# A gated long-convolution and MLP stack: an on-chip re/im swap issued by one engine's DMA queue instead of two, with a new instruction plan

## The chip, the cores and the metric

The kernel runs on one core of one Trainium2 chip. A core has five engines with an in-order instruction stream each: TensorE (PE in the profile, with its weight loads as PEld), VectorE (DVE), ScalarE (ACT), GpSimd (POOL) and SyncE (SP). They share one on-chip memory of 128 partitions (SBUF, here one array called `ar` and a small one called `sm`), and the matmul accumulators (PSUM, `ps`, used as eight banks of 512 f32 per partition). Engines wait for each other through semaphores. Copies between memories, and copies within the on-chip memory, are DMAs: an instruction in an engine's stream issues them, and they then run beside the engines. The metric is the device time of one execution in microseconds.

## The reference

The sequence has 2048 tokens of 512 channels, in bf16; the MLP's hidden size is 1376. Cut to what matters:

```python
def A(q, k, v, shift_k, ssm_k, ssm_D):      # gated long convolution
    k_shift = sum(k_pad[:, t:t+S] * shift_k[:, 3-t] for t in range(4))   # causal, 4 taps
    kv = k_shift * v
    y = irfft(rfft(pad(kv, 2*S)) * rfft(pad(ssm_k, 2*S)))[:S]            # causal, 2048 taps
    return q * (y + kv * ssm_D)
def B(x):                                   # MLP
    return gelu(layernorm(x) @ w1 + b1) @ w2 + b2

x = q
x = x + A(layernorm(x), k, v, shift_k, ssm_k, ssm_D)
x = x + B(layernorm(x))
x = x + A(layernorm(x), k, v, shift_k, ssm_k, ssm_D)
x = x + B(layernorm(x))
```

Only the gate `q` differs between the two uses of A, so the convolution's result is computed once and used in both layers.

## The kernel before, in words

**The planner.** The program is written as a list of operations. `P.op` records each with the engine or engines that may run it, an assumed duration, what it reads and writes, and its PSUM tiles. `schedule` (L188) then places them one after another on the five engines in a modelled time: by a priority, which is the length of the work that follows, plus a stage's boost, plus a table of per-operation corrections ("nudges", at the end of the kernel function). Where an operation allows ACT or DVE, as PSUM evacuations and layer norms do, this choice is made there too, and so is the PSUM bank. The result is a fixed order for each engine. `sync` adds the semaphore waits that this order needs, and `emit` writes the streams. So an assumed duration or a nudge is no instruction, but it can change where any instruction stands. For DMAs the planner keeps one time, `dma_free`, at which the shared DMA engines are done with what was issued, at an assumed 400 bytes per ns (L289, L290).

**The convolution.** The sequence is cut into two halves of 1024 tokens. Each half and each half of the convolution kernel is transformed by a two-stage Fourier transform done as matmuls against tables: `stage1` (L627) and `stage2` (L641), each group of matmuls followed by an evacuation from PSUM (L541 on ACT, L542 on DVE). In a spectrum, 64 partitions hold real parts and 64 hold imaginary parts. A complex product needs each spectrum also with the two exchanged. For the convolution kernel's spectra this exchange is done by DVE copies, `swap_v` (L666). For the spectrum of the second half's `kv` it is done by DMAs, `swap` (L646 to L651): C5 is copied to C1 with partitions 0 to 63 and 64 to 127 exchanged, in two pieces of the channel axis, and in two directions for each piece, thus four DMAs of 0.5 MB, all issued through `dma` (L522). The direction `h` picks the issuing engine: SP for `h` = 0, ACT for `h` = 1. The spectral products follow on DVE (`tt`, L531): for the second half a loop over four groups, in which C5 and then C1 is multiplied by C3 and added to C6 and C4. `inverse1` (L679) and `inverse2` (L694) transform back. The short convolution is done on PE for the first half (`taps`) and on DVE for the second (`shift`).

**The MLP blocks.** The two layers run in eight blocks of 512 tokens, k = 0 to 7. In (layer, token group) they are (0,0), (0,1), (1,0), (1,1), (0,2), (0,3), (1,2), (1,3): the first half of the sequence goes through both layers before the second half, so blocks 0 to 3 run while the second half's convolution is still being computed between them. A block has four tiles of 128 tokens. For each tile there are statistics on DVE (L884, L886) with a small power on POOL (L892), a norm on ACT (L931) or DVE (L932), the product with y and the addition to x (L974, L975, shown under the line of `tt`), the statistics and a norm again, and a transpose that brings channels onto partitions. Block 0 transposes on PE. Blocks 1 to 7 use one transposing DMA for each tile, issued by SP (L986), 28 in all. Then come the first matmuls (L1009) in eleven slices of the hidden size, with a gelu on ACT for each slice (L1014), the second matmuls (L1029) for each tile, and the addition to x on DVE (L1033). The outputs leave by DMAs on SP.

So SP's stream holds the loads, then the transposes of each block, with two of the four swap DMAs among them, and then the outputs. ACT's stream holds evacuations, norms and gelus, with the other two swap DMAs among them.

Of the kernel before, what the change touches and what calls it, by code (L numbers as in the profile page):

```python
# [7 lines left out]
ALU = mybir.AluOpType  # L8
# [37 lines left out]
class Prog:  # L46
# [141 lines left out]
    def schedule(self, nudge={}):  # L188
# [32 lines left out]
        while done < n:  # L221
# [64 lines left out]
                left -= k  # L286
            free[e] = s + d
            if o.dma:
                dma_free = max(dma_free, s + d) + o.bytes / 400.0  # L289
                o.end = dma_free + (1900.0 if o.dma is True else o.dma)  # L290
            else:
                o.end = s + d
            for tl in o.tile:
# [122 lines left out]
                getattr(block, e)(body)  # L416


WF, SPL, NA1, NDX, KP, KM, SG, PG, PSW, PLN, END = 8, 1, 0, 64, 2, 0, 1, 1, 0, 0, 1
S, D, FF = 2048, 512, 1376  # L420
B = 1024
EPS = 1e-5
# [39 lines left out]
def bass_interleave_layers__ssm_conv_h3__mixer_channel_mlp__prompt_kernel(  # L462
        nc, A_q, A_k, A_v, A_shift_k, A_ssm_k, A_ssm_D, B_x, B_w1, B_b1, B_w2, B_b2, out):
    P = Prog(nc)
# [5 lines left out]
    def A(p0, n, off, *dims):  # L470
        return bass.AP(ar, p0 * AR + off, [[AR, n]] + [list(d) for d in dims])
# [4 lines left out]
    def Q(tile, p0, n, off, *dims):  # L476
        return bass.AP(ps, p0 * 4096 + tile.base * 512 + off, [[4096, n]] + [list(d) for d in dims])
# [43 lines left out]
    def dma(dst, src, nbytes, reads=(), prio=0.0, writes=None, eng=SP):  # L521
        return P.op(eng, lambda e: e.dma_start(dst, src, allow_slow_non_contiguous=True), 550.0, reads=reads,  # L522
                    writes=[dst] if writes is None else writes, dma=True, nbytes=nbytes, prio=prio, order=HOLD[0])
# [6 lines left out]
    def tt(o, a, b, op, dur, eng=DVE):  # L530
        return P.op(eng, lambda e: e.tensor_tensor(o, a, b, op), dur, reads=[a, b], writes=[o])  # L531
# [114 lines left out]
    def swap(dst0, src0, dg0=0, nd=64):  # L646
        out = []
        for h in range(2):
            s = A(64 * h, 64, src0 + dg0 * 128, [1, nd * 128])
            out.append(dma(A(64 - 64 * h, 64, dst0 + dg0 * 128, [1, nd * 128]), s, nd * 37500, reads=[s], eng=(SP, ACT)[h]))  # L650
        return out  # L651

    def W32(p0, n, off, nd, nk):
# [14 lines left out]
    def DG(r, g):  # L668
        return A(0, 128, r + 2048 * g, [1, 2048])

    def inverse1(p1, p2, z, hf, d8s):
        for d8 in d8s:
            tl = Tile(cv[hf], 0, hi[hf])
            ins = [(i, j, A(0, 128, p + (8 * d8 + i) * 128, [1, 128]), A(0, 128, R_U + 128 * j, [1, 128]))
                   for i in range(8) for j, p in enumerate((p1, p2))]

            def f(e, ins=ins, tl=tl):
                for i, j, w, m in ins:
                    r = e.matmul(Q(tl, 0, 128, i * 128, [1, 128]), w, m, start=j == 0, stop=j == 1)  # L679
                return r  # L680
            P.op(PE, f, 16 * 57.0, reads=[x for y_ in ins for x in y_[2:]], tile=tl, ni=32)
            evac(A(0, 128, z + 1024 * d8, [8, 8], [64, 16], [1, 8]),
                 lambda tl=tl: Q(tl, 0, 128, 0, [128, 8], [8, 16], [1, 8]), tl)

    def inverse2(z, y, hf):
        nd = 512
        for a2, na in [(0, 1), (1, 1)] * (NA1 > hf) + [(i, 2) for i in range(NA1 > hf, 4)]:
            tl = Tile(one if na == 1 else cv[hf], 0, hi[hf])
            ins = [(i, ri, A(0, 128, R_T2 + ((na * a2 + i) * 2 + ri) * 128, [1, 128]),
                    A(0, 128, z + ((na * a2 + i) * 2 + ri) * 64, [1024, 8], [1, 64])) for i in range(na) for ri in range(2)]  # L690

            def f(e, ins=ins, tl=tl):
                for i, ri, w, m in ins:
                    r = e.matmul(Q(tl, 0, 128, i * nd, [1, nd]), w, m, start=ri == 0, stop=ri == 1)  # L694
                return r
            P.op(PE, f, 2 * na * nd * 0.422, reads=[x for y_ in ins for x in y_[2:]], tile=tl, ni=4 * na)
            evac(A(0, 128, y + a2 * na * 512, [512, na], [1, nd]), lambda tl=tl, na=na: Q(tl, 0, 128, 0, [nd, na], [1, nd]), tl,
                 dur={ACT: 475.0, DVE: 630.0} if na == 1 else EVD)
# [130 lines left out]
    stage1([(R_H0, 0), (HT1, 256)], R_SH, 1, range(8))  # L829

    P.boost, EV[0] = FIRST, (ACT, DVE)
    inverse1(C1, C4, C6, 0, range(8))
    inverse2(C6, YS[0], 0)


# [18 lines left out]
        stage2(C1, C5, 1, g)  # L854
    for i in range(2):
        swap(C1, C5, 32 * i, 32)
    for g in range(4):
        for i, (p, x) in enumerate(((C6, C5), (C4, C1))):
            m = A(0, 128, R_H0 + 2048 * i, [1, 2048])
            tt(m, DG(x, g), DG(C3, g), ALU.mult, 1133.0)  # L860
            tt(DG(p, g), DG(p, g), m, ALU.add, 1133.0)
    inverse1(C6, C4, C1, 1, range(8))
    inverse2(C1, YS[8], 1)


    EV[0] = (ACT, DVE)
# [86 lines left out]
    for L, b in [(0, 0), (0, 1), (1, 0), (1, 1), (0, 2), (0, 3), (1, 2), (1, 3)]:  # L953
# [8 lines left out]
        bo = dict(P.boost)  # L962

        def lean(i):
            P.boost = {e: bo[e] + (3e5 if k < SPL and i < 2 else 0.0) for e in bo}
        for i, s in enumerate(sl):
            lean(i)
            zt = zts[i]
# [2 lines left out]
            if i % 2:  # L971
# [1 line left out]
                x2 = A(0, 128, XS[s - 1], [1, 1024])  # L973
                tt(z2, z2, A(0, 128, YS[s - 1], [1, 1024]), ALU.mult, 610.0)  # L974
                tt(x2, x2, z2, ALU.add, 610.0)  # L975
        lean(0)
        mr = stats(sl[:2], True, k > 0)
        lean(2)
        mr = mr + stats(sl[2:], True, k > 0)
        for i, s in enumerate(sl):  # L980
            lean(i)
            z = ntmp()
            norm(s, mr[i], A(0, 128, z, [1, 512]))
            if k not in BYPE:
                zs, xt = A(0, 128, z, [1, 512]), A(0, 128, R_XT + (k % 2) * 2048 + i * 128, [512, 4], [1, 128])
                P.op(SP, lambda e, zs=zs, xt=xt: e.dma_start(xt, zs, transpose=True), 1200.0, reads=[zs], writes=[xt],  # L986
                     dma=1250.0, nbytes=1000)
                continue
            tl = Tile(ptr, lo)
            src = [A(0, 128, z + 128 * j, [1, 128]) for j in range(4)]  # L990

            def f(e, src=src, tl=tl):
                for j in range(4):
                    r = e.transpose(QB(tl, 0, 128, 128 * j, [1, 128]), src[j], IDN)
                return r
            P.op(PE, f, 4 * 60.0, reads=src + [IDN], tile=tl, prio=2e5, ni=8)
            evac(A(0, 128, R_XT + (k % 2) * 2048 + i * 128, [512, 4], [1, 128]),
                 lambda tl=tl: QB(tl, 0, 128, 0, [128, 4], [1, 128]), tl, dur={ACT: 510.0, DVE: 360.0})
        P.boost = bo
        nt = 256 if k < SPL else 512  # L1000
        for t0, fc in [(t0, fc) for t0 in range(0, 512, nt) for fc in range(11)]:
            rows = 128 if fc < 10 else 96
            tl = Tile(pm1, lo)
# [36 lines left out]
                o = (b // 2) * B * 512 + (s % 8 - 1) * 512  # L1040
                outs.append(dma(dr(out, o, [8 * 512, 128], [1, 1024]), src, 1 << 18, reads=[src], writes=[]))
    P.schedule({
        4: -2722000, 5: -2787700, 6: -1724800, 7: -1209900, 9: -3195100, 10: -2512200, 11: -3537200, 12: -9892100,
        13: -3275900, 14: -2545200, 15: -1219700, 17: -1775500, 18: -4912800, 50: 1831800, 51: 669200, 53: 971300,
        59: 177000, 60: -127200, 63: 78900, 64: -2944000, 69: 1351300, 71: 2209900, 72: 1484900, 73: 364500,
        75: 4879100, 83: -6452800, 87: -79900, 89: -6939400, 100: -473600, 109: 505300, 112: -1220500, 130: -292500,
        139: 2217400, 144: 726100, 146: 725300, 148: 104200, 150: 46100, 152: 701300, 156: 809900, 157: 79000,
        159: 809400, 160: 1509400, 161: 1511900, 181: 2148200, 182: -4908700, 208: -675200, 216: -541300,
        217: -635900, 218: -377200, 219: -300000, 231: -2087100, 232: -1420500, 236: -1145000, 238: -1105300,
        239: -323000, 263: 1329100, 286: -314700, 323: -3260500, 325: -4484200, 333: -695800, 337: -731700,  # L1050
        358: -186700, 364: 881800, 371: 845700, 374: 5603900, 376: 7181700, 378: 5920300, 380: 8518000,
        383: -2852800, 388: 4950600, 390: 9651700, 392: 6143000, 394: 5859400, 400: -256900, 402: -359100,
        404: 4316100, 406: 4317000, 408: -231500, 410: 4127200, 412: 4968900, 416: 2718700, 420: -567700,
        423: -882600, 428: 1119900, 430: -113000, 432: -196900, 434: -57500, 445: -1125900, 449: -3768000,
        450: -1182200, 459: -2467500, 469: -1401400, 485: 614700, 487: 240000, 489: 615700, 491: 251700,
        500: -685500, 501: -2286200, 505: 413200, 508: -715300, 524: -461900, 525: -358200, 559: -2269500,
        560: -2008000, 562: -2155300, 564: -2546100, 576: 2300300, 577: 3514400, 578: 3193800, 580: 4805700,
        585: 2437100, 586: 4776600, 587: 5927400, 589: 4099400, 641: -1729200, 645: -2893000, 649: 1567700,
        675: -1125900, 750: -4094700, 758: -8732500, 795: -16699900, 797: -15253500, 799: -7825800, 801: -4476400,
        803: -19174100, 805: -16887100, 807: -13420200, 809: -14748800, 811: -13422400, 813: -13127700,  # L1060
        815: -11697300, 821: -6064400, 909: 673900, 991: -10275500})
    P.sync()
    P.emit(outs)

# [27 lines left out]
```

## Time and profile before

| | us |
|---|---|
| device time, four runs | 249.57, 251.95, 251.08, 252.67 |
| median | 251.52 |
| the profiled execution, device time | 249.57 |
| its span in the profile | 247.5 |
| evacuations on ACT (L541), 91 | 87.9 |
| gelus on ACT (L1014), 99 | 61.1 |
| norms on ACT (L931), 28, and on DVE (L932), 36 | 21.8 and 13.9 |
| elementwise products on DVE (L531), 76 | 77.0 |
| first and second MLP matmuls on PE (L1009, L1029) | 78.8 and 78.1 |
| swap DMA, issue to landing, median, from SP and from ACT | 7.4 and 9.1 |
| transposing DMA (28), issue to landing, median | 2.5 |

The profile is of one execution. Its granted clock is 1.0 throughout. Times inside it are microseconds from the span's start. Letters stand for engines as above; SPq and ACTq are the streams of SP and ACT with the DMAs that they issue; `ar<-ar` is a DMA or an operation within the on-chip memory, `ps` is PSUM. A group line gives the operation, its count, busy time and the mean of one in ns, and then the engine's idle time just before the group's instructions with what ended most of it.

### The profile page before, as it was taken

The numbers are of one execution on the slowest core, as the hardware profiler recorded it, in microseconds if no ns is written. First come the engines' busy times: TensorE is split into PE (matmuls) and PEld (weight loads), VectorE is DVE, ScalarE is ACT, GpSimd is POOL, SyncE is SP. The second block draws the span as 40 slices with busy tenths as digits, with TensorE's granted clock in tenths as the row PEclk, the third lists the DMA queues.
The fourth block names the chain that finished last, engine by engine and source line by source line (L and its number), as shares of the span: only waits on it lengthen the run. The fifth ranks groups of instructions, "written<-read, shape, count | busy, mean of one in ns | idle before, by whom it ended". The sixth has DMA issues, their size and how long they took to land.

```text
span 247.5 us, 5560 instructions
## 1 busy us (share of the span) xinstructions
PE 234.4 (95%) x2380; PEld 141.6 (57%) x2404; DVE 193.3 (78%) x362; ACT 167.9 (68%) x219; POOL 26.9 (11%) x32
## 2 busy tenths in 40 slices
PE   7999987999799999999699999999999999999995
PEld 4777776896587654456344576444444444444443
DVE  3698999999999999899999998889146966942022
ACT  3497789999999887867685399836804823743810
POOL 0001100000412010402113003111101011020000
PEclk9999999999999999999999999999999999999999
DMA  6999990604001430002692400052400030033002
GB/s 187 375 422 415 402 302 15 236 15 162 3 3 21 171 64 3 0 3 48 151 226 45 119 11 0 3 109 62 85 3 0 1 73 12 3 64 106 0 3 85
DMA packets 22097, 24.78 MB, mean 100 GB/s; under 512 B 15956, under 2 KB 17849, under 8 KB 20665
## 3 DMA queue, kind: packets, MB, share of 16 engines
q1 hardware_dynamic: 21752, 23.34, 29.8%
q10 hardware_dynamic: 320, 1.09, 1.9%
q8 instruction: 19, 0.31, 0.5%
q14 instruction: 6, 0.04, 0.0%
HBM read 16.56 MB, written 2.10 MB: 75 GB/s over the span
## 4 chain that ended last, share of the span: by engine, by line
PE 81%; ACT 11%; DVE 4%; issue 1%; DMA 1%
PE ps L1009 31%; PE ps L1029 30%; ACT ar L541 11%; PE ps L641 4%; PE ps L627 4%; PE ps L679 3%; PE ps L606 2%; PE ps L568 2%; PE ps L694 1%; DVE ar L542 1%; PE ps L759 1%; PE ps L765 1%; DMA ar<-ar 1%; DVE ar L611 1%; PE ps L586 1%
## 5 line engine op out<-in xcount | busy, mean ns | idle before, releaser
L541 ACT ACTIVATE ar<-ps 128x1024 bf16<-128x1024 f32 (+2 forms) x91 | 87.9, 1028 | 20.5 <-PE ps L641 5.6
L1014 ACT ACTIVATE ar<-ps,sm 128x512 bf16<-128x512 f32 (+2 forms) x99 | 61.1, 640 | 40.8 <-PE ps L1009 40.2
L1009 PE MATMUL ps<-ar 128*128 128x512 bf16 (+3 forms) x387 | 78.8, 355 | 2.5 <-DMA ar<-ar 2.0
L531 DVE TENSOR_TENSOR ar<-ar 128x2048 bf16<-128x2048 bf16 (+2 forms) x76 | 77.0, 1049 | 2.7 <-ACT ar L541 1.9
L1029 PE MATMUL ps<-ar 128*128 128x512 bf16 (+2 forms) x351 | 78.1, 372 | 0.7 <-issue 0.2
L1009 PEld LDWEIGHTS ps<-ar 128*128 128x128 bf16 (+1 forms) x396 | 38.8, 100 | 37.7 <-DMA ar<-ar 1.9
L1029 PEld LDWEIGHTS ps<-ar 128*128 128x128 bf16 (+1 forms) x363 | 34.8, 98 | 38.1
L1033 DVE TENSOR_TENSOR ar<-ar,ps 128x512 bf16<-128x512 bf16 (+1 forms) x33 | 21.7, 668 | 33.6 <-PE ps L1029 33.5
L892 POOL TENSOR_TENSOR sm<-sm 128x2 f32<-128x2 f32 (+1 forms) x24 | 25.4, 1060 | 178.3 <-DVE sm L891 177.8
L884 DVE BATCH_NORM_STATS2 sm<-ar 128x6 f32<-128x512 bf16 x64 | 42.3, 682 | 0.3
L931 ACT ACTIVATE ar<-ar,sm 128x512 bf16<-128x512 bf16 x28 | 21.8, 808 | 4.8 <-DMA ar<-ar 2.0
L627 PE MATMUL ps<-ar 128*64 128x128 bf16 x640 | 22.4, 221 | 1.5 <-ACT ar L541 1.0
L627 PEld LDWEIGHTS ps<-ar 128*64 128x64 bf16 x640 | 18.6, 110 | 6.7 <-issue 2.6
L641 PE MATMUL ps<-ar 128*128 128x64 bf16 x512 | 18.6, 193 | 3.6 <-ACT ar L541 1.9
L641 PEld LDWEIGHTS ps<-ar 128*128 128x128 bf16 x512 | 16.8, 98 | 7.4 <-ACT ar L541 3.7
L679 PE MATMUL ps<-ar 128*128 128x128 bf16 x256 | 15.6, 219 | 0.2 <-DVE ar L531 0.2
L679 PEld LDWEIGHTS ps<-ar 128*128 128x128 bf16 x256 | 14.7, 98 | 1.8 <-DVE ar L531 0.4
L932 DVE TENSOR_SCALAR ar<-ar,sm 128x512 bf16<-128x512 bf16 x36 | 13.9, 414 | 1.0 <-DMA ar<-ar 0.5
L666 DVE COPY ar<-ar 64x2048 bf16<-64x2048 bf16 x16 | 10.9, 688 | 0.4
L886 DVE BATCH_NORM_AGGREGATE sm<-sm 128x2 f32<-128x6 f32 x64 | 10.2, 174 | 0.4
L542 DVE CAST ar<-ps 128x1024 bf16<-128x1024 f32 x8 | 9.7, 1217 | 0.1
L694 PE MATMUL ps<-ar 128*128 128x512 bf16 x32 | 7.9, 380 | 0.0
(33 smaller groups left out, 64.9 us busy)
## 6 DMA issues: line engine op xcount, KB each, us to landing
ar<-tab_s SPq DMA_DIRECT2D x4, 1024.0 KB, 18.1
ar<-in_A_ssm_k_dram SPq DMA_DIRECT2D x4, 512.0 KB, 6.7
ar<-in_A_q_dram SPq DMA_DIRECT2D x2, 1024.0 KB, 6.0
ar<-in_A_v_dram SPq DMA_DIRECT2D x2, 1024.0 KB, 10.0
out_dram<-ar SPq DMA_DIRECT2D x7, 256.0 KB, 2.2
ar<-in_A_k_dram SPq DMA_DIRECT2D x1, 1408.0 KB, 7.6
ar<-in_B_w_dram SPq DMA_DIRECT2D x1, 1376.0 KB, 22.1
ar<-in_B_w_dram SPq DMA_DIRECT2D x1, 1280.0 KB, 23.0
```

The source lines that it names most:

```text
L531: return P.op(eng, lambda e: e.tensor_tensor(o, a, b, op), dur, reads=[a, b], writes=[o])
L541: return e.activation(dst, src(), AF.Copy)
L627: r = e.matmul(Q(tl, 64 * ri, 64, i * 128, [1, 128]), w, m, start=j == 0, stop=j == len(terms) - 1)
L641: r = e.matmul(Q(tl, 0, 128, i * nd, [1, nd]), w, m, start=True, stop=True)
L679: r = e.matmul(Q(tl, 0, 128, i * 128, [1, 128]), w, m, start=j == 0, stop=j == 1)
L884: P.op(DVE, lambda e, st=st, x=x: e.bn_stats(st, x), 630.0, reads=[x], writes=[st])
L892: P.op(POOL, lambda e: e.tensor_tensor(r, v, h, ALU.pow), 1200.0, reads=[v, h], writes=[r])
L931: return e.activation(o, x, AF.Identity, bias=mr[2], scale=mr[1])
L1009: r = e.matmul(Q(tl, 0, rows, 0, [1, nt]), w, m, start=dk == 0, stop=dk == 3)
L1014: P.op(ACT, lambda e, dst=dst, tl=tl, rows=rows, bias=bias, nt=nt: e.activation(dst, Q(tl, 0, rows, 0, [1, nt]), AF.Gelu_apprx_tanh, bias= ...
L1029: r = e.matmul(Q(tl, 0, 128, 0, [1, n]), ins[fc][0], ins[fc][1], start=fc == 0, stop=fc == 10)
L1033: P.op(DVE, lambda e, x=x, tl=tl, n=nc2: e.tensor_tensor(x, x, Q(tl, 0, 128, 0, [1, n]), ALU.add), 85.0 + nc2 * 1.055, reads=[x], writes=[ ...
```

## The change

The swap's `h` = 0 direction goes to ACT too, so that all four swap DMAs are issued by ACT, and SP issues only the transposes, besides loads and outputs. In the planner's model, a DMA marked 1251.0 instead of 1250.0 neither waits for nor adds to `dma_free`; the transposes are so marked. The table of nudges is a new one throughout, so the plan is made anew: the order on each engine, and for some operations the choice between ACT and DVE. `inverse1` takes its spectra as a tuple; called with two, it issues what it issued before. The switches `IA` and `ST4` are 0 and `SPS` is (0,), with which the added branches issue what the code before issued.

```diff
@@ schedule
             if o.dma:
-                dma_free = max(dma_free, s + d) + o.bytes / 400.0
-                o.end = dma_free + (1900.0 if o.dma is True else o.dma)
+                if o.dma == 1251.0:
+                    o.end = s + d + o.dma
+                else:
+                    dma_free = max(dma_free, s + d) + o.bytes / 400.0
+                    o.end = dma_free + (1900.0 if o.dma is True else o.dma)
...
-WF, SPL, NA1, NDX, KP, KM, SG, PG, PSW, PLN, END = 8, 1, 0, 64, 2, 0, 1, 1, 0, 0, 1
+WF, SPL, NA1, NDX, KP, KM, SG, PG, PSW, PLN, END, SPS, ST4, IA, SWA = 8, 1, 0, 64, 2, 0, 1, 1, 0, 0, 1, (0,), 0, 0, 1
...
@@ swap
-            out.append(dma(A(64 - 64 * h, 64, dst0 + dg0 * 128, [1, nd * 128]), s, nd * 37500, reads=[s], eng=(SP, ACT)[h]))
+            out.append(dma(A(64 - 64 * h, 64, dst0 + dg0 * 128, [1, nd * 128]), s, nd * 37500, reads=[s], eng=(ACT if SWA else SP, ACT)[h]))
...
@@ transposes of the MLP input
                 P.op(SP, lambda e, zs=zs, xt=xt: e.dma_start(xt, zs, transpose=True), 1200.0, reads=[zs], writes=[xt],
-                     dma=1250.0, nbytes=1000)
+                     dma=1251.0 if SWA else 1250.0, nbytes=1000)
...
@@ P.schedule({ ... }), first lines of the table
-        4: -2722000, 5: -2787700, 6: -1724800, 7: -1209900, 9: -3195100, 10: -2512200, 11: -3537200, 12: -9892100,
+        4: -2868200, 5: -1791300, 8: 340900, 9: -3663100, 10: -643600, 11: -4939200, 12: -9800600, 13: -5002900,
...
```

## The prediction

> **What bounds the kernel now.** I read the page's busy times, then a table of windows, then the chain of work, then each queue's own timeline where the chain leaves the matmuls.
>
> ```profile
> PE 234.4 (95%) x2380; PEld 141.6 (57%) x2404; DVE 193.3 (78%) x362; ACT 167.9 (68%) x219; POOL 26.9 (11%) x32
> ...
> 10.00:42.00 32.00, 29.53 (x641) 24.49 (x643) 29.93 (x52) 26.86 (x29) 2.18 (x3) 1.00 0.85 328
> 42.00:69.00 27.00, 24.24 (x525) 20.02 (x523) 26.63 (x37) 27.00 (x29) 3.57 (x4) 1.00 0.28 95
> 69.00:118.00 49.00, 48.01 (x503) 29.87 (x507) 46.91 (x82) 40.89 (x63) 6.89 (x6) 1.00 0.16 41
> 118.00:154.00 36.00, 33.75 (x255) 19.41 (x257) 35.11 (x66) 25.77 (x36) 5.97 (x5) 1.00 0.39 92
> 154.00:247.00 93.00, 90.45 (x424) 42.47 (x430) 51.03 (x121) 44.13 (x64) 8.02 (x10) 1.00 0.17 40
> ```
>
> The windows give length, then busy us of PE, PEld, DVE, ACT and POOL, the clock, and DMA. PE looks busy everywhere, but from 42 to 69 us ACT is busy for 27.00 of 27.00 and DVE for 26.63: those two set the pace there. DVE stays above 95% until 154. From 154 to the end it has slack, and PE alone decides. So a delay in what DVE or ACT must finish before an MLP block moves the end; after that only PE's own gaps count. The chain shows one gap, just where block 2 (the first after both halves of token group 0 are done) begins:
>
> ```profile
> 117.12 0.36 DVE ar L1033
> 117.47 2.48 DMA ar<-ar
> 119.95 0.27 issue
> 120.23 9.45 PE ps L1009 x43
> ```
>
> The change speaks of the DMA queues, so I read SP and ACT around it:
>
> ```profile
> 113.61 5.12 SPq L986 DMA_TRANSPOSE ar<-ar  x4
> 119.55 1.17 SPq L522 DMA_DIRECT2D ar<-ar  x2
> 132.38 5.12 SPq L986 DMA_TRANSPOSE ar<-ar  x4
> ...
> SPq L986 <- ACT ar L931: 13.3, 2, 12.3
> ...
> 119.56 1.83 ACTq L522 DMA_DIRECT2D ar<-ar  x2
> 121.44 0.69 ACT L1014 ACTIVATE ar<-ps,sm 128x512 bf16<-128x512 f32 x1 [1.91 <-PE ps L1009]
> 122.02 0.80 ACT L931 ACTIVATE ar<-ar,sm 128x512 bf16<-128x512 bf16 x1
> ...
> L522 SPq DMA_DIRECT2D ar<-ar x2: 543/565/587, 119.5 to 120.1; - x2
> L522 ACTq DMA_DIRECT2D ar<-ar x2: 535/898/1260, 119.6 to 120.1; - x2
> ```
>
> Block 2's four transposes stand before the swap on SP. They are 1.28 us apart because SP issues them one after another (5.12 us for four), and the last lands 2.5 us after its issue: 117.45 + 2.5 = 119.95, which is the gap. The next four, block 3's, stand behind the swap, but SP waited 12.3 us for ACT's norm (L931), long after its two swap issues were over at 120.7. **The swap delays no transpose here.** ACT is the opposite: its first gelu of block 2 starts at 121.44, right behind its two swap issues, though its matmuls were done before.
>
> [...] four 0.5 MB pieces from two queues took up to 11.1 us to land, with the DMA engines 94% busy from 120 to 130. So I give the queue itself no bandwidth. [...]
>
> **The change, part by part.** I take the instruction order of both programs. The new switches (SPS, ST4, IA) stand at values that issue what was issued before, and the planner's case 1251 acts only through the order it gives. Operations and their number are the same, except that three norms (L931/L932) move from DVE to ACT, one stage-1 evacuation from ACT to DVE, and one small K evacuation back.
>
> 1. *Two swap issues leave SP* (0.57 us each). SP then waited 12.3 us anyway: gain 0. If that cover went, 1.2 us.
>
> 2. *Two more swap issues go on ACT*, four in a row, behind block 2's first gelu. Two took 1.83 us. Four cost between 4 x 0.57 = 2.3 us (SP's pace) and 4 x 1.31 = 5.2 us (ACT's slower one, with the gap to the next instruction). I take S = 3.0: the slow one came while SP was issuing too, which it no longer does. Queued behind them on ACT are the other ten gelus of block 2 and block 3's first norm. The matmul group of each hidden slice takes 0.86 us. The waits of the new program let six groups run before the seventh needs the second gelu. The last swap source evacuation ends, by step 4, some 1.3 us after block 2's first matmul; then gelu 0.6, the issues S, gelu 0.67 and about 0.15 of signalling: the second gelu is seen at 1.3 + 0.6 + 3.0 + 0.8 = 5.7 us, against six groups, 5.2. PE waits 0.5 to 0.6 us (0 for S = 2.3; 2.8 for 5.2). Before, it waited 0.2 here. Net **+0.4**.
>
> 3. *A new order up to 69 us.* Nothing is added but 0.7 us more on DVE (evacuation 1.12 to 1.2 in, norms 0.33 each and small evacuations about the same out). K arrives one 1 MB table later, about 2.5 us at 410 GB/s, and PE has 48 more stage-1 matmuls ahead of it. Charging each DVE instruction what it took before, DVE starts the spectral products at about 42.0 against 41.89. ACT then has 26.7 us to the first MLP evacuation, as before. **0**, within 1.5 either way.
>
> 4. *When block 2 can start.* Three things must be there. (a) DVE's last addition of block 1 (L1033), which frees a PSUM bank: 106.25 us of DVE work lie ahead of it before, and it started at 117.12, so DVE had paused 10.9 us in all; 108.37 us lie ahead in the new order, as bn_stats of blocks 4 and 5 (0.60 each) are pulled forward. With 10.4 us of pauses (its last 0.34 wait goes) it starts at 118.8 and ends at 119.4. (b) The transposes: the second statistics pass of block 2 lies behind 103.65 instead of 102.46 us of DVE work; ends 114.2; two norms on ACT (0.72 each) to 115.8; the chain on SP began at 113.6, four by 1.28, last landing 119.9. (c) ACT: five stage-2 evacuations (0.92 each) now follow those norms: 115.8 + 4.6, with two waits on PE about 121.5, which lets PE's last stage-2 group go at 120.1. So block 2 starts near 120.1 to 120.3. The 2.0 us gap stays in another form. **+0.1**.
>
> 5. *Block 3.* DVE can take block 3's first product (L974) only when ACT has given the norm behind the swap issues. Sum from block 2's start: norm at 6.4, then 7.4 us of DVE work, the addition of block 2, scale and norm, four transposes 1.28 apart and 2.5 to land: 21.3 us. PE has 19.0 us of block 2, 0.6 of step 2, and two inverse groups (0.89 each) that the new order puts ahead: 21.4. A tie, before it was one too (138.7 against 138.81). I allow **+0.3**. The swap's data: first pair issued by 123.3, landing by 132 at the measured rate (before: 2.1 MB in 11.1 us, 190 GB/s); DVE asks for it at 134. Hidden; without the 2 us of cover it would add one for one.
>
> 6. *From block 3 on* PE has the same matmuls in nearly the same order: **0**.
>
> Sum: +0.4 + 0 + 0.1 + 0.3 = **+0.8 us**. The profiled execution took 249.57 with a span of 247.5, so 250.4 for the like; it was the lowest of four, and the median, 251.52, becomes **252.3**.
>
> **Rivals.**
> - *Faster: DVE pauses less.* DVE paused 4.5 us from 9.65 to 117. If it paused only half as much, (a) gives 117.4, the transposes 117.8, and PE's own work 117.5 to 118: block 2 starts 2.2 us sooner, while step 2 takes 0.4 back: 249.7. For it: a fresh plan. Against it: it gives DVE 2.1 us more ahead of the block. Since blocks 2 to 7 need 125 us of PE, over 1% of gain has no place in the trace.
> - *Slower: the four issues hold ACT.* Same place as step 2: PE waits for the second gelu, DVE for the norm, and the transposes of block 3 follow. Each us over S = 3.0 costs one. At 5.2, +3.0: 254.5. It decides (over 1%) from S = 4.7. For it: the 1260 ns issue. Against: three issues of 535 to 587.
> - *Slower: DVE pauses more.* Nearly every instruction in 42 to 118 is now placed just behind its input (the copies at L666 need the last evacuation of the kernel's spectrum, which ACT now does after several gelus). 2.2 us more of pauses: block 2 at 122.3, 254.5.
> - *The queue move does nothing by itself.* That is part of my forecast: steps 1 and 3 to 5 would hold with the swap left on both queues.
>
> **Numbers.** Forecast 0.50 (own range 250.8 to 254.0, bounds of S from 2.3 to 4.5 and pauses by 1 us), faster rival 0.15, ACT held 0.12, DVE pausing more 0.23. One per cent, about what a measurement of this kernel can tell from no change, is 2.5 us. Faster by over 1%: the tail of the second, 0.06. Slower by over 1%: most of the last two and a sixth of the first, 0.36. The rest, 0.58. The range goes from 249.3 to 256.0.
>
> **What the new profile would show.** Four ACT-issued copies in a row, 2.3 to 3.7 us, with the second gelu and the norm behind; PE's wait at the seventh group of block 2; block 2's first matmul at 120 to 121 with less than 2 us before it but idle bits spread before; transposes of block 3 landing within 1 us of their use; ends of blocks 4 to 7 unchanged. The prediction is wrong if block 2 begins outside 118.5 to 121.5, or if PE shows new gaps after block 3.

## The result and the profile after

The changed kernel takes 252.63 us (median), the kernel before 250.62 beside it: 1.0049 of before, 95% interval 1.0029 to 1.0068, thus 1.2 us more (0.0049 x 250.6). For these runs that ratio is also the ratio of the means; the medians lie 2.0 us apart. In both kernels the runs fall into two groups by the clock granted over the span: in experiment 1 the changed kernel and the one before have medians of 250.64 and 250.37 us at a clock of about 1.0, and of 253.31 and 252.25 us at 0.986 to 0.993, where 11 of 20 and 24 of 51 of their runs lie. The forecast was +0.8 us and "within 1%". The size is right, but the parts are not: two of them were wrong by more than a microsecond each, with opposite signs.

The first profiled execution (253.36 us, span 251.5) was among the longer ones of its program. A second profile of the same program, 250.54 us with a span of 248.7, is the one to read beside the profile before (249.57, 247.5): in the first, one small load landed late (at 5.50 us) and VectorE's first evacuation began at 10.76 us, against 9.60 in the second and 9.65 before. What follows from 119 us on is the same in both, shifted. The chain of waits of the first profile around block 2, with start, length and what it was:

```profile
119.26 3.77 ACT ar L544 x4
123.03 0.54 ACT ar L1027
123.61 0.60 ACTq L525
124.25 1.87 ACTq L525
126.15 2.17 ACTq L525
128.37 0.70 ACT ar L1027
129.11 4.49 PE ps L1022 x20
```

The chain runs through the swap's issues. Here are the timelines of the second profile: SP, then ACT, then PE, with start, length, engine and line, and in brackets the idle time before and what ended it.

```profile
112.36 28.50 SPq L999 DMA_TRANSPOSE ar<-ar  x8
...
120.10 0.71 ACT L1027 ACTIVATE ar<-ps,sm 128x512 bf16<-128x512 f32 x1
120.27 5.27 ACTq L525 DMA_DIRECT2D ar<-ar  x4
125.59 0.69 ACT L1027 ACTIVATE ar<-ps,sm 128x512 bf16<-128x512 f32 x1 [4.78 <-issue]
126.18 0.80 ACT L941 ACTIVATE ar<-ar,sm 128x512 bf16<-128x512 bf16 x1
...
118.46 0.64 PE L644 MATMUL ps<-ar 128*128 128x64 bf16 x16 [0.27 <-ACT ar L544]
118.94 5.34 PE L1022 MATMUL ps<-ar 128*128 128x512 bf16 x24
126.33 4.49 PE L1022 MATMUL ps<-ar 128*128 128x512 bf16 x20 [2.05 <-ACT ar L1027]
```

Block 2 begins at 118.94, where it began at 120.23 before, and the 2.0 us gap ahead of it is gone. But the four issues keep ACT for 5.27 us, the second gelu waits behind them, and TensorE pauses 2.05 us for it after six slices. The windows of the second profile (length, then busy us of PE, PEld, DVE, ACT, POOL, then clock and DMA) agree:

```profile
42.00:69.00 27.00, 24.03 (x507) 19.82 (x505) 26.66 (x34) 26.74 (x29) 1.66 (x1) 1.00 0.28 95
69.00:118.00 49.00, 48.59 (x516) 30.05 (x516) 47.73 (x88) 42.12 (x67) 8.07 (x8) 1.00 0.18 44
118.00:154.00 36.00, 33.67 (x270) 19.20 (x267) 33.02 (x60) 24.47 (x35) 5.34 (x4) 1.00 0.38 89
```

From 69 to 118 us DVE is busy 47.73 us, where it was 46.91: it pauses less. From 118 to 154 DVE and ACT are busy for 2.1 and 1.3 us less than before. ACT is held up by its issues; in experiment 2, without them, it is busy for 26.84 us there. DVE's fall isn't the pause, since experiment 2 has DVE at 33.12 as well: a part of its work now lies ahead of 118 us.

### The profile page after: what moved, and what is told of

It reads as the page before. It is cut to its first block, busy times and chain, and to the rows that moved or that the text cites. A ratio compares the mean times of both kernels' runs of the same rounds, so it can differ in the third digit from the quotient of the medians.

```text
span 251.5 us, 5560 instructions
## 1 busy us (share of the span) xinstructions
PE 235.1 (93%) x2381; PEld 142.0 (56%) x2404; DVE 192.3 (76%) x359; ACT 167.7 (67%) x222; POOL 27.0 (11%) x32
## 4 chain that ended last, share of the span: by engine, by line
PE 68%; DVE 13%; ACT 11%; DMA 3%; ACTq 2%; issue 1%
PE ps L1022 28%; PE ps L1042 27%; ACT ar L544 9%; DVE ar L534 7%; PE ps L682 4%; ACTq L525 2%; PE ps L644 2%; DVE ar L545 2%; PE ps L630 2%; DMA ar<-ar 2%; DVE ar L669 2%; DMA ar<-in_A_ssm_D_dram 1%; PE ps L697 1%; PE ps L609 1%; PE ps L571 1%
## 5 line engine op out<-in xcount | busy, mean ns | idle before, releaser
L544 ACT ACTIVATE ar<-ps 128x1024 bf16<-128x1024 f32 (+2 forms) x91 | 86.9, 1036 | 26.9 <-PE ps L630 6.9
L941 ACT ACTIVATE ar<-ar,sm 128x512 bf16<-128x512 bf16 x31 | 24.1, 810 | 8.0 <-DVE sm L904 5.9
L942 DVE TENSOR_SCALAR ar<-ar,sm 128x512 bf16<-128x512 bf16 x33 | 12.6, 406 | 0.7 <-DMA ar<-ar 0.4
L545 DVE CAST ar<-ps 128x1024 bf16<-128x1024 f32 x9 | 10.7, 1218 | 0.9 <-PE ps L630 0.5
L904 DVE SCALAR_TENSOR_TENSOR sm<-sm 128x2 f32<-128x2 f32 (+1 forms) x21 | 3.2, 154 | 6.6 <-POOL sm L902 6.6
```

Source lines behind the costliest of these rows:

```text
L544: return e.activation(dst, src(), AF.Copy)
L941: return e.activation(o, x, AF.Identity, bias=mr[2], scale=mr[1])
```

## The experiments

Most edits keep the planned orders and move single operations. A helper does it after the planning and before the waits are made: `put(E, a, i...)` takes operations `i` out of their engine's order and puts them on engine `E` behind operation `a`. Operations 285 to 288 are the swap: 285 and 286 are the two directions of the first piece, 287 and 288 those of the second.

**1. The changed kernel again.** No edit; this is the second profile above.

> The changed kernel once more, for a second profile. The first profiled execution took 253.36 us, 4.0 us over the profiled one of before, while the medians differ by 2.0 us only. If the issue theory holds, the four swap issues on ScalarE take about 5.3 us again and the first matmuls of block 2 pause for about 2.0 us at the seventh slice. The late start of the first profile (a small load landed at 5.5 us, 1.3 us later than before) is expected to be gone in a run near 250.6 us and to be there again in a run near 253 us.

It took 252.71 us, 1.003 of before (1.000 to 1.006). Issues 5.27 us, pause 2.05, and the late start absent from the 250.54 us execution: as expected. Whether the late start belongs to the runs near 253 us wasn't seen, as only one execution was profiled. The times of the one program reach from 250.2 to 255.1 us, 14 of 22 above 251.5; of before 20 of 51.

**2. One direction back on SyncE**, in the changed kernel's plan: the queue move undone alone.

```diff
+    put(SP, 553, 285, 287)
```

> The changed kernel with every order as it is, only the two swap issues of direction 0 put back on SyncE behind block 2's transposes. Issue theory: two issues on ScalarE take 1.2 to 1.9 us, the second gelu comes 3.4 us sooner, the pause of the matmuls in block 2 falls from 2.0 to at most 0.3 us, and the time is 1.7 to 2 us below the changed kernel's on this chip. Plan theory (the new order is what costs, the swap's queue nothing): within 0.5 us of the changed kernel.

It took 248.59 us, **0.9924 of before** (0.9895 to 0.9952). Its ACT and PE timelines:

```profile
120.14 0.71 ACT L1027 ACTIVATE ar<-ps,sm 128x512 bf16<-128x512 f32 x1
120.30 1.83 ACTq L525 DMA_DIRECT2D ar<-ar  x2
122.18 0.69 ACT L1027 ACTIVATE ar<-ps,sm 128x512 bf16<-128x512 f32 x1 [1.33 <-PE ps L1022]
...
118.97 9.66 PE L1022 MATMUL ps<-ar 128*128 128x512 bf16 x44
```

Until 120.3 us ACT and DVE start each instruction within 0.1 us of experiment 1's profile. Then the second gelu comes 3.41 us sooner, all 44 matmuls of block 2 run without a pause, and block 7 begins at 224.81 instead of 226.98, 2.17 us sooner. On the same chip the queue move costs 1.003 / 0.9924, that is 1.07% or 2.7 us, and the rest of the change gains 0.76%, 1.9 us. Among the runs at a clock of 1.0 alone the medians are 248.57 here, 250.64 with the queue move and 250.37 before: the move costs 2.1 us, which is the pause, and the rest gains 1.8. The other 0.6 us of the 2.7 are runs at a lower clock, 11 of 20 with the move and 1 of 14 here. The plan theory falls for the loss, and the new plan is shown to be better than the old one.

**3. The kernel before, all four issues on ScalarE**: the queue move done alone in the old plan.

```diff
+    put(ACT, 284, 285, 286, 287, 288)
```

> The kernel before with every order as it is, only the two swap issues of SyncE put on ScalarE beside the other two, ahead of block 2's first gelu. Issue theory: four issues take 5.3 us instead of 1.83, the first gelu starts near 124.8 instead of 121.4, three PSUM banks run out at 122.8, so the matmuls pause for 2 to 2.5 us, and block 3's chain is 3.4 us later: 2 to 3.5 us slower than before. Plan theory: within 0.5 us of before.

It took 254.09 us, 1.0127 of before (1.0088 to 1.0165), 3.2 us more, as the issue theory said. But all six runs had a clock of 0.986 to 0.993, and against the runs of before at such a clock (252.25) it is 1.8 us more, so a part of the 3.2 us goes with the clock. ACT, then PE:

```profile
120.80 5.27 ACTq L522 DMA_DIRECT2D ar<-ar  x4
126.12 0.69 ACT L1014 ACTIVATE ar<-ps,sm 128x512 bf16<-128x512 f32 x1 [5.35 <-issue]
...
121.29 4.45 PE L1009 MATMUL ps<-ar 128*128 128x512 bf16 x12 [1.85 <-DMA ar<-ar]
126.87 1.04 PE L1009 MATMUL ps<-ar 128*128 128x512 bf16 x4 [1.13 <-ACT ar L1014]
```

The issues take 5.27 us here too. The pause behind three slices is only 1.13 us, not 2 to 2.5; the twelve matmuls ahead of it took 4.45 us, where twelve take 2.75 in experiment 8, and the granted clock was 0.50 from 122 to 124 us (see there).

**4. The kernel before, all four issues on SyncE.**

```diff
+    put(SP, 549, 285, 286, 287, 288)
```

> The kernel before with every order as it is, only the two swap issues of ScalarE put on SyncE behind the other two. Issue theory: block 2's first gelu starts about 0.4 us sooner (when its matmuls are done) and ScalarE has 1.8 us less; SyncE issues four in 2.3 us and has 9 us to spare; the time is 0 to 0.5 us lower, since the matmuls hardly waited there. Plan theory: the same as before within 0.5 us. A copy slowed by one queue would show as VectorE waiting for a swap past 134 us: up to 2 us slower.

It took 250.27 us, 1.0004 of before (0.9978 to 1.003). SP's timeline:

```profile
120.12 5.29 SPq L522 DMA_DIRECT2D ar<-ar  x4
132.66 5.12 SPq L986 DMA_TRANSPOSE ar<-ar  x4
```

SP needs 5.29 us for the four, not the expected 2.3, as ACT needs 5.27; one by one 0.55, 0.59, 1.86 and 2.17. So ACT is not slower at issuing these copies than SP: four in a row into one queue take 5.27 us on ACT and 5.29 on SP. On SP that harms nobody, since block 3's transposes are not due until 132.66.

**5. The second pair late**, all four still on ScalarE.

```diff
+    put(ACT, 571, 287, 288)
```

> The changed kernel with all four swap issues still on ScalarE, but the second pair moved behind the last gelu of block 2, when the first pair has landed. In the runs so far the four issues of one queue took 0.5, 0.6, 1.9 and 2.2 us, on ScalarE and on SyncE alike. Full-queue theory (an issue is slow while its queue still holds the earlier copies): each of the four now takes 0.5 to 0.6, or up to 1.3 for a second one; the second gelu comes about 1.2 us behind the first; the matmuls do not pause in block 2; the time is within 0.5 us of the kernel with one direction put back on SyncE, 2 to 2.7 us below the changed kernel. Per-issue theory (the third and fourth issue cost 2 us wherever they stand): the late pair takes 4 us, hidden from the gelus but ahead of block 3's norms on ScalarE; block 3 starts 1 us or more later. VectorE needs the second pair at about 141 us; issued near 130 it has 11 us to land.

It took 249.17 us, 0.9942 of before (0.9917 to 0.9967). The ACT timeline:

```profile
120.51 1.15 ACTq L525 DMA_DIRECT2D ar<-ar  x2
121.71 0.69 ACT L1027 ACTIVATE ar<-ps,sm 128x512 bf16<-128x512 f32 x1 [0.66 <-PE ps L1022]
...
128.88 0.47 ACTq L525 DMA_DIRECT2D ar<-ar  x1
...
129.38 0.61 ACTq L525 DMA_DIRECT2D ar<-ar  x1
```

The same four issues on the same engine now take about 0.5 to 0.6 us each, and the loss is gone. The per-issue theory falls: what was slow is an issue close behind two others in its queue. In experiment 1 the third and the fourth took 1.87 and 2.19 us, and as no copy landed in less than 4.5 us from its issue, none had landed before 124.77, when the third was over (123.33) and the fourth under way. That it is the queue, and not only the load on the DMA engines, experiment 2 shows: there the same four copies, issued within 1.9 us from two queues, took 2.9 us of issues in all, where one queue took 5.2.

**6. Three issues on ScalarE, one on SyncE.**

```diff
+    put(SP, 553, 287)
```

> The changed kernel with three of the four issues left on ScalarE and one (direction 0 of the second pair) on SyncE. Full-queue theory: the three take 0.5 + 0.6 + 1.9 = 3.0 us, just the sum S that the forecast took for four. With two (1.84 us) the matmuls did not pause, with four (5.26 us) the time was 2.2 us longer, so 1.2 us of the issues' time is covered beyond two. At 3.0 us the matmuls pause for 0 to 0.6 us (the forecast's own estimate for S = 3.0), and the time is within 0.6 us of the kernel with one direction put back. Per-issue theory: the same sum, so it is told apart by the run before this one, not here. If the time is half-way between (1.1 us up), the cover was misjudged.

It took 250.06 us, 0.9983 of before (0.9958 to 1.0008): between experiment 2 (0.9924) and the changed kernel (1.003), and higher than expected. ACT, then PE:

```profile
120.55 3.81 ACTq L525 DMA_DIRECT2D ar<-ar  x3
124.41 0.69 ACT L1027 ACTIVATE ar<-ps,sm 128x512 bf16<-128x512 f32 x1 [3.31 <-PE ps L1022]
...
125.15 4.49 PE L1022 MATMUL ps<-ar 128*128 128x512 bf16 x20 [0.59 <-ACT ar L1027]
```

The third issue took 2.6 us, not 1.9. SP's copy ran beside; whether that made the issue longer, no run tests. With the runs above there are now four points. Issues of 1.83, 3.81 and 5.27 us gave pauses of 0, 0.59 and 2.05; experiment 10 adds 2.85 us with 0. **In these four the pause is what the issues take beyond 3.2 us.** That is the arithmetic of step 2 with one term struck: the last evacuation ends 1.3 us after block 2's first matmul, then S, then a gelu of 0.7 with 0.05 us before it and 0.05 behind it (experiment 1; the forecast put 0.15), against six slices in 5.3. The first gelu (0.6 in the forecast) isn't in the row, since the issues begin while it still runs (120.27, gelu from 120.10 to 120.81).

**7. All four on SyncE in the changed kernel's plan.**

```diff
+    put(SP, 553, 285, 286, 287, 288)
```

> The changed kernel's plan with all four swap issues on SyncE behind block 2's transposes. Issue theory: SyncE takes 5.3 us for the four, from 120.3 to 125.6, and has until 133.5; ScalarE loses its last two issues, but with two the matmuls already ran without a pause: within 0.5 us of the kernel with one direction put back, so about 0.8% below before. If VectorE's first product of block 3 waits on ScalarE's norm behind the two issues, up to 0.7 us less than that. If one queue carries the copies more slowly, VectorE waits at 132.6 for the first pair: up to 2 us more.

It took 249.15 us, 0.9946 of before (0.992 to 0.9972), no different from experiment 2 or 5 by their intervals. As ScalarE's issues get shorter than 3.2 us nothing more is gained: experiment 5, on the same chip, took 249.17.

**8. The kernel before with its gap filled**: ten matmuls of constants just ahead of block 2's first.

```diff
+    def cover(e):
+        for i in range(10):
+            r = e.matmul(bass.AP(ps, 7 * 512, [[4096, 128], [1, 512]]), IDN, A(0, 128, R_F, [1, 512]), start=True, stop=True)
+        return r
...
+    P.order[PE].insert(next(n for n, o in enumerate(P.order[PE]) if o.i == 554), g)
```

> The kernel before with ten matmuls of constants (128x512 each, into a PSUM bank that nothing uses then, result not read) put into TensorE's 2.0 us gap ahead of block 2. They add work and should gain nothing by themselves: at most 0.2 us more. In the runs so far the times of before fall into two groups: granted clock 1.0 over the span (27 runs, median 250.4) and 0.986 to 0.993 (24 runs, 252.3), and a profile of the second sort shows the clock at 0.50 just as block 2 begins, after a pause. Pause theory (a pause of TensorE ahead of block 2 brings the clock down, and a part of the changed plan's gain is a shorter pause): the runs at 0.993 or lower fall from about half to under a fifth and the median goes to 250.3 to 250.6. Chance theory (the dips have nothing to do with the gap): about half again and the same two medians.

It took 250.25 us, 0.9969 of before (0.9944 to 0.9994). So ten useless matmuls made the kernel no slower and by the interval 0.06 to 0.56% faster. The medians are alike (250.19 before); the gain is that the long runs are gone. None of 22 runs was above 251.04 us; 25 of 75 of before beside it were above 251.5. The expectation missed in one point: 7 runs, not under a fifth, had a clock of 0.993 over the span, but they took 250.3 to 250.5 us. That fits a fall of the clock which is cheap elsewhere and dear at block 2: experiment 10's profiled run has 0.993 over the span, 1.00 in every window of 2 us from 116 to 132, and took 248.81 us. The only other profiled run at 0.993 is experiment 3's, and there the fall is at block 2, by windows of 2 us:

```profile
118.00:120.00 2.00, 1.44 (x34) 1.07 (x32) 1.66 (x4) 1.91 (x3) 0.00 (x0) 1.00 0.35 70
120.00:122.00 2.00, 0.71 (x3) 0.36 (x4) 1.87 (x7) 0.77 (x1) 1.01 (x1) 0.93 0.40 82
122.00:124.00 2.00, 2.00 (x6) 0.73 (x5) 2.00 (x5) 0.00 (x0) 0.00 (x0) 0.50 1.15 233
124.00:126.00 2.00, 1.74 (x6) 0.43 (x4) 0.48 (x2) 0.00 (x0) 0.00 (x0) 0.72 0.89 225
```

The column before the DMA share is the granted clock: 0.50 from 122 to 124 us, just after a pause of 1.85 us, with six matmuls in 2 us instead of the eleven that the profile before has in that window at 1.00. That the pause brings the clock down was not shown: the profile before has a pause of 2.04 us at the same place and a clock of 1.0 throughout.

**9. Experiment 2 with the loads in the old order.**

```diff
+    put(SP, 553, 285, 287)
+    P.order[SP][:15] = [P.ops[i] for i in (8, 16, 7, 6, 15, 4, 5, 17, 10, 14, 9, 13, 11, 18, 12)]
...
```

> The changed kernel with one direction of the swap back on SyncE, and its first fifteen loads in the order of the kernel before (k ahead of the first 1 MB table, the small table ahead of v). It tests step 3 of the forecast, which gave the new load order 0 within 1.5 us. If step 3 holds: within 0.7 us of the same kernel with the new load order (run beside it here). If the new load order is what makes the plan better: 1 us or more slower than that, VectorE's first spectral product later than 42.5 us. If the old order is the better one: VectorE starts the products near 41.5 and the time falls by up to 1 us.

It took 250.22 us, 0.9961 of before (0.9942 to 0.998); experiment 12, the same with the new loads on the same chip, took 248.92. Each of its 22 runs is longer than each of the 8 there. So the new load order is worth about 1.3 us in the new plan, and even without it the kernel is faster than before. VectorE's timelines from 40 us show where. First with the old order, then with the new one:

```profile
44.14 2.36 DVE L534 TENSOR_TENSOR ar<-ar 128x2048 bf16<-128x2048 bf16 x2 [0.20 <-ACT ar L544]
```

```profile
42.76 3.50 DVE L534 TENSOR_TENSOR ar<-ar 128x2048 bf16<-128x2048 bf16 x3 [0.20 <-ACT ar L544]
```

With the old order the first spectral product starts 1.38 us later, and that stays to the end.

**10. Copies of half the size.** The copies take the first half of their channels only; half of the swap is left out. All orders stay as they are.

```diff
-            s = A(64 * h, 64, src0 + dg0 * 128, [1, nd * 128])
+            s = A(64 * h, 64, src0 + dg0 * 128, [1, nd * 64])
```

(and the same for the destination)

> The changed kernel, all four swap issues on ScalarE in place, but each copies only the first half of its channels (0.25 MB instead of 0.5 MB; half of the swap is left out, nothing else). If an issue is slow because of what its queue still has to carry: four issues in 2.0 to 3.2 us, no pause or a short one (0 to 0.1 us) of the matmuls in block 2, and the time as with one direction back on SyncE (about 0.6% below before). If the number of copies in the queue decides: 5.3 us again and the changed kernel's time. In between, 3.2 us is the length from which the matmuls pause by what four and three issues showed (5.27 gave 2.05, 3.81 gave 0.59).

It took 249.07 us, 0.9918 of before (0.9889 to 0.9947). ACT, then PE:

```profile
120.73 2.85 ACTq L525 DMA_DIRECT2D ar<-ar  x4
...
119.39 9.66 PE L1022 MATMUL ps<-ar 128*128 128x512 bf16 x44
```

Four issues in 2.85 us, where four of the full size took 5.27, and no pause. Their number is the same, so it is the size of what the queue has to carry, not the count of copies, that made the issues slow here. Whether bytes count there, or the pieces into which a copy is split, was not told apart.

**11. The changed kernel with its pause partly filled**: eight such matmuls of constants ahead of the seventh slice.

```diff
...
+    P.order[PE].insert(next(n for n, o in enumerate(P.order[PE]) if o.i == 568), g)
```

> The changed kernel with eight matmuls of constants (128x512, into an unused PSUM bank, result not read) ahead of the seventh slice's matmuls of block 2, where TensorE pauses 2.05 us. They take nothing away from the pause. In the changed kernel 27 of 44 and 14 of 22 runs took more than 251.5 us, at a granted clock below 0.995 in nearly all. Pause theory: such runs fall to under a fifth, the median goes to 250.4 to 250.9, and the ratio to before to 0.997 to 1.002. Chance theory: half or more again, median 252 to 253.

It took 251.36 us, 1.0002 of before (0.9972 to 1.0032), with 7 of 14 runs above 251.5 and the longest 252.5. The expectation missed: the longer runs did not go, only those of 253 us and more did, and five of the seven had a clock of 1.0. Its profile still has a gap of 0.33 us behind the filler. So filling the gap removes the long runs of the kernel before (experiment 8), but that it does so through the clock was not shown; what spreads the changed kernel's times isn't settled.

**12. Experiment 2 again.**

> The changed kernel with one direction of the swap back on SyncE, once more on this chip, beside the others. 0.990 to 0.996 of before; TensorE without a pause in block 2; no run over 251.5 us.

It took 248.92 us, 0.991 of before (0.9875 to 0.9945), no run above 249.6. With experiment 2 it is faster than both kernels, twice.

## Why the prediction was right, and where it was not

The total came out, +1.2 us for a forecast of +0.8, because two errors nearly cancelled. That it came out so close is luck in a second way: the forecast was worked out on a profile with a clock of 1.0, and among runs at that clock the change costs about 0.3 us (9 runs, 250.64, against 27, 250.37), the sum of 1.8 gained by the plan and 2.1 lost by the queue move. The rest of the 1.2 are runs at a lower clock, of which the forecast says nothing.

1. *Issues leave SP, gain 0*: right. In every profile block 3's transposes wait for norms, and in experiment 4 SP carried four issues at no cost.

2. *Four issues on ACT, S = 3.0, net +0.4*: **this step failed in its size.** S is 5.27, at the upper end of the range (5.2), and the pause is 2.05 us; in whole runs the queue move cost 2.7 us. The forecast took the slow second issue (1260 ns) for a clash with SP's issuing, which would go away, and it did: with one queue issuing alone the second issue took 0.6 us (experiments 1, 4 and 5), and with two at once ACT's second issue took 1.26 again in experiment 2, but ACT's two took 1.27 in all in experiment 8 and 1.17 in 12. What the forecast had wrong is the third and the fourth issue, which it priced like the first two. They took 1.87 and 2.18 close behind the first two, of which none had landed before the third was over; 8 us behind them they took 0.47 and 0.61 (experiment 5), and at half the size all four took 2.85 (experiment 10). The profile before has a sign of it, and I passed over it. SP's timeline, where the last of the big table loads is issued behind the others:

```profile
7.47 5.35 SPq L528 DMA_DIRECT2D ar<-tab_s  x1
```

This one issue lasts 5.35 us, where the two table loads before it took 0.91 together. The rival "the four issues hold ACT" had the right S, the right place and the right wait. It got S by luck, as four issues of 1.31 us, where they took 0.5, 0.6, 1.9 and 2.2. It priced S = 5.2 at 2.8 us of pause (its own sum gives 2.7) and got 2.05, because of the first gelu that it counted in.

3. *The new order up to 69 us, 0*: right as a sum. The first spectral product starts at 42.49 in the second profile (forecast 42.0, before 41.89). The profile before is an early one: in the other three of the old plan (experiments 3, 4, 8) it starts at 43.14, 42.45 and 43.17. What was not seen is that the new load order carries 1.3 us of it: without it the new plan starts at 44.1 (experiment 9).

4. *Block 2's start, +0.1*: **failed, by 1.3 us.** It begins at 118.94, not at 120.1 to 120.3. Of its three conditions the addition was put at 118.8 and came at 117.59, and the transposes were to begin at 113.6 and began at 112.36. DVE paused 9.8 us in all ahead of that addition, where the forecast took 10.4 and before had 10.87; its work ahead was 107.8 us, 0.6 less than charged. So the rival "DVE pauses less" had the direction, and 1.3 of its 2.2 us. But the addition isn't what let block 2 start sooner: it comes later than before (117.59, before 117.12). Before, block 2 waited for its last transpose, which landed at 119.95; in the second profile that lands at 118.69, and block 2 follows a stage-2 group of matmuls without a gap. So what gains is that the new order brings the transposes sooner. From the first spectral product to block 2 it takes 76.4 us in nine of the ten profiles of the new plan (77.6 in the first), 78.2 to 78.3 in all four of the old one: 1.8 us, with the new loads and with the old. Experiment 2 shows the same in whole runs, 1.8 to 1.9 us. Which of the moved operations does it, no run shows. Of the forecast's own signs of being wrong none came true in the second profile (118.94 lies within 118.5 to 121.5, and TensorE has no new gap behind block 3); in the first, with its late load, block 2 begins at 121.73, just outside.

5. *Block 3, +0.3*: right. From block 2's first matmul to block 4's it takes 48.81 us in experiment 2, against 48.40 before. VectorE waits for no swap in any profile.

6. *From block 3 on, 0*: right. From block 4's first matmul to block 7's it takes 57.03 us, before 57.04.

Between the second profile and the one before, at block 4's first matmul: -1.29 for the block's earlier start, +2.05 for the pause and +0.56 for the rest make +1.32, which is 169.95 against 168.63. Since the profile before is an early one, this pair shows less of the plan's gain than the whole runs do.

The forecast gave the queue itself no bandwidth, and that held: from the first issue to the last landing the four copies took 12.3 us from one queue (first profile) and 12.1 from two (experiment 2). What differed is the time of the issuing engine, 5.27 us with one queue against 1.83 on ACT with two, and the pause that it made is the loss.

## What to carry to other kernels

The price of a DMA for its issuing engine wasn't a constant here: an issue of the same 0.5 MB copy took from 0.47 to 2.19 us. Look in the profile for the longest issue of its kind, and ask what was issued into its queue just before. Where the engine had work behind it, three ways kept the pause away: the issues spaced by 8 us (experiment 5: 0.47 and 0.61 us each), smaller copies (10: 2.85 us for four) and a second queue (2: 1.83 us on ACT). A long row did no harm on an engine that had time, as SP had here (5.29 us, experiment 4). A sum that comes out proves no term of it: undo one part alone, which here split a change of 0.3% on one chip into a gain of 0.8% and a loss of 1.1%.

## What the runs showed of the hardware that I had not expected

- Four 0.5 MB copies within the on-chip memory, issued in a row into one queue, took 0.5, 0.6, 1.9 and 2.2 us to issue, on ScalarE (experiment 1) and on SyncE (experiment 4) alike; at half the size 2.85 us for the four (experiment 10); with the second pair 8 us later 1.15 us for the first two, then 0.47 and 0.61 (experiment 5).
- With two queues issuing such copies at once, ScalarE's second issue took 1.26 us in the profile before and in experiment 2, where alone it took 0.6; in experiments 8 and 12 ScalarE's two took 1.27 and 1.17 us in all.
- The first DMA issue on ScalarE began while the activation ahead of it still ran (0.54 us of overlap in the second profile).
- Ten matmuls without use in a gap of 2.0 us left no run above 251.1 us, where a third of the runs of the kernel before lay above 251.5; the medians are alike (250.25 and 250.19), and the ratio is 0.9969.
